# Wider, differently paced weight conversions, and an SBUF copy under the second ELU half, in a float32 attention and two-MoE kernel

## The chip, the cores and the metric

The kernel runs on one core of one Trainium2 chip. The metric is the device time of one execution in microseconds (us). Runs of the same kernel are compared by their median.

## The reference, cut to what matters

Three blocks follow each other: a linear attention, an MLP with an ELU, and a mixture of four experts with a ReLU. All are float32; the two ELU weights `w_in` and `w_out` come as 64-bit floats and are converted on the chip.

```python
def phi(x):                                   # 4 batches, 8 heads, 576 rows, 64 -> 128 features
    proj = einsum('bhsd,df->bhsf', x, w_phi)
    proj = proj - max(abs(proj), axis=-1)
    return concatenate([exp(proj), exp(-proj)])
num = phi(q) @ (phi(k)^T v);  den = phi(q) @ sum(phi(k)) + 1e-6
x = num / den                                 # as 2304 rows of 512
h = x @ w_in                                  # 512 -> 2048
x = where(h > 0, h, exp(min(h, 0)) - 1) @ w_out
for e in range(4):                            # w1: 512 -> 1024, w2: 1024 -> 512
    out += p[:, e] * (maximum(x @ w1[e], 0) @ w2[e])
```

## The kernel before, in words

Every float32 product is made of three products of a rounded high part and a low part (`hi*hi`, `hi*lo`, `lo*hi`), which ScalarE (a copy to the type fp32r) and VectorE or GpSimd (a subtraction) split off. Names of engines below: PE is TensorE, DVE is VectorE, ACT is ScalarE, POOL is GpSimd, SP issues the DMAs.

**Stage 1, attention, ELU first half and conversions** (to about 461 us). `attention` (L344) runs 16 pairs of heads as generators (`pair`, L175), several in flight. For each pair DVE makes two projections safe (`guard`, L205: a reduction L208 and a subtraction L209; the results for q are the tiles `qd0` and `qd1`), PE transposes them (L248), ACT takes exponentials, PE forms `kv` and `num`, DVE divides (a reciprocal L329 and products L332). The first half of the 2048 ELU features is done in 9 tiles of 256 rows by 4 units (`Elu`, L491: first product L503 to L505, ELU L511 to L516, second product L532 to L534).

In the same stage `convert64` (L99) turns `w_in` and `w_out` from 64-bit floats into float32, 32 tiles of 128x512: it loads 64-bit words into the tile `w64` (L101), takes absolute values on ACT (L107), clamps, shifts, and rebuilds the high word on DVE (L109 to L111), makes a power of two from it on DVE (L112, tile `pw`), scales the low word on ACT (L113, tile `low`), multiplies and adds on POOL (L115, L117). The 16 tiles of the first half are split into high and low parts (L121, L123); the 16 tiles of the second half are written to DRAM (`wscr`, L119) and read back later. A block is 256 columns (`CVW`), so there are 64 blocks. The pool `cv` has three buffers of each tile (`CVB`), so up to three blocks are in flight; the buffer of `w64` comes free for the next load when L111 and L113 have read it.

**What sets the order.** The generator `weight_stream` (L413) advances the blocks in flight by one step per call. `drive` and `slot` (L736, L751) call it `wrate` times at each of four points of an ELU unit, and the loop at L763 calls it `PRE` times per attention step; `need_w` forces what is due. The resulting program order is a priority: a scheduler of the framework then places the instructions of each engine, taking into account which buffers are free. On the chip each engine runs its own queue strictly in that order.

**Stage 2, ELU second half** (about 461 to 676 us). The second half of the features is done with a seven-product (Winograd) form of 2x2 blocks on groups of 768 rows (`Up`, L614). Each `UpElu` (L667) forms sums of PSUM banks and kept copies: `middle` and `end` write the sum of a kept copy and a bank back into the bank (L647, L664), or into the SBUF tile `c22` (L656), or use the bank as it is (L662); `half` (L668) then reads this sum twice: ACT makes `relu(-c)` and `exp` in the tile `te` (L671, L672), DVE makes `max(te - 1, c)` (L673), ACT and DVE split it into `h` (L674, L675). The bank is in use until L673 has read it. PSUM has eight banks; four to eight of them hold the sums of `Out` (L678, L696 to L698).

**Stage 3, experts** (676 us to the end). The same `Up` with a ReLU (`half`, L632), and `Down` (L704) for the second product.

Of the kernel before, what the change touches and what calls it, by code (L numbers as in the profile page):

```python
# [19 lines left out]
P = 128  # L20
# [13 lines left out]
TC = 384  # L34
# [8 lines left out]
ATT_LAG = 5  # L43
PRE = 2
RATE = 1.4
# [3 lines left out]
ATE = 6  # L49
WFAST = 4  # L50
TEB = 2
PB = 4
EL = 'V'
NF32 = 7
LDB = 1
CVP = 16
CVW = 256
CVOFF = 0
# [5 lines left out]
def attn_elu_moe_kernel(ctx: ExitStack, tc: tile.TileContext, kq_in, vv, w_phi, w_in, w_out, probs, w1, w2, out):  # L64
# [34 lines left out]
    def convert64(dst, src, adder):  # L99
# [4 lines left out]
        top = cv.tile([P, CVW], U32, tag="top", name="top")  # L104
        pw = cv.tile([P, CVW], U32, tag="pw", name="pw")
        low = cv.tile([P, CVW], F32, tag="low", name="low")
        A.activation(f32(top), f32(hi), ACTF.Abs)  # L107
# [3 lines left out]
        V.scalar_tensor_tensor(out=top, in0=hi, scalar=0xC0000000, in1=top, op0=ALU.bitwise_and, op1=ALU.bitwise_or)  # L111
        V.tensor_scalar(out=pw, in0=top, scalar1=0xFF800000, scalar2=None, op0=ALU.bitwise_and)  # L112
        A.activation(low, lo, ACTF.Copy, scale=2.0 ** -52)  # L113
        yield
        G.tensor_tensor(out=low, in0=low, in1=f32(pw), op=ALU.mult)  # L115
        yield
        adder.tensor_tensor(out=f32(top), in0=f32(top), in1=low, op=ALU.add)  # L117
        if dst.dtype == F32:
# [495 lines left out]
    class Up:  # L614
# [16 lines left out]

        def half(self, c, s, f):  # L632
            h = hp.tile([P, 2, TC], F32R, tag="h", name="h", bufs=HB)
            A.activation(h[:, 0], c, ACTF.Relu)  # L634
            V.scalar_tensor_tensor(out=h[:, 1], in0=c, scalar=0.0, in1=f32(h[:, 0]), op0=ALU.max, op1=ALU.subtract)  # L635
            hs[s, f] = h
# [6 lines left out]
        def middle(self):  # L643
            q = self.q
            b2 = bank()[:, :TC]
            self.product(b2, 2, 2)
            V.tensor_tensor(out=b2, in0=self.m, in1=b2, op=ALU.add)  # L647
            self.half(b2, 0, q)
            self.product(self.b1, 3, 4, True)
            self.ma = self.keep(self.b1, "cma")  # L650
            self.b3 = bank()[:, :TC]
            self.product(self.b3, 4, 3)
            self.product(self.b1, 1, 1, True)
            mab = self.keep(self.b1, "cmab")
            c22 = hp.tile([P, TC], F32, tag="c22", name="c22", bufs=1)
            V.tensor_tensor(out=c22, in0=mab, in1=self.b3, op=ALU.add)  # L656
            self.half(c22, 1, q + NQ)

        def end(self):
            q = self.q  # L660
            self.product(self.b1, 5, 5, True)
            self.half(self.b1, 0, q + NQ)  # L662
            self.product(self.b3, 6, 6, True)
            V.tensor_tensor(out=self.b3, in0=self.ma, in1=self.b3, op=ALU.add)  # L664
            self.half(self.b3, 1, q)

    class UpElu(Up):  # L667
        def half(self, c, s, f):  # L668
            h = hp.tile([P, 2, TC], F32R, tag="h", name="h", bufs=HB)
            t = bp.tile([P, TC], F32, tag="te", name="te", bufs=TEB)  # L670
            A.activation(t, c, ACTF.Relu, scale=-1.0)  # L671
            A.activation(t, t, ACTF.Exp, scale=-1.0)  # L672
            V.scalar_tensor_tensor(out=t, in0=t, scalar=1.0, in1=c, op0=ALU.subtract, op1=ALU.max)  # L673
            A.activation(h[:, 0], t, ACTF.Copy)  # L674
            on[EL].tensor_tensor(out=h[:, 1], in0=t, in1=f32(h[:, 0]), op=ALU.subtract)  # L675
            hs[s, f] = h
# [59 lines left out]
    def slot():  # L736
        quota[0] += rate[0]
        while quota[0] >= 1:
            quota[0] -= 1
            if done[0] < limit[0]:  # L740
                next(stream, None)
        for _ in range(wrate[0]):
            next(weights, None)

    wrate = [WRATE]
    quota = [0.0]
# [21 lines left out]
    for t, u in order(TAIL):  # L768
        if u == 0:
# [3 lines left out]
            limit[0] = NP * (t // 2 + 2)  # L773
            rate[0] = RATE if t < ATE else 0.0
            if t == ATE:
                att.close()
# [164 lines left out]
```

## Time and profile before

| | us |
|---|---|
| median of 3 runs (lowest, highest) | 1435.88 (1433.95, 1436.28) |
| the profiled execution's own time | 1437.87 |
| span of the profiled execution | 1436.1 |
| PE busy | 1376.5 |
| DVE busy | 751.3 |
| ACT busy | 644.1 |
| POOL busy | 448.9 |

The span runs from the first to the last instruction. A wait is listed as who waited, on which line, for whom; the share of busy time of an engine is given for stretches of the span. PE's rows are its matmuls, PEld's are the weight loads, which overlap them.

### The profile page before, as it was taken

The page shows a single profiled execution, that of the slowest core. Times are in us where ns is not written, and L with a number is a line of the kernel's source. Part 1 is how long each engine was busy: PE and PEld are TensorE (multiplying, and loading weights), DVE is VectorE, ACT ScalarE, POOL GpSimd, SP SyncE. Part 2 cuts the span into 40 slices and gives each one's busy share as a digit, 9 for nine tenths or more (in the row PEclk, how much of TensorE's full clock was granted, in tenths as well). Part 3 has the DMA queues.
Part 4 walks back from the last instruction along what each step waited for, and adds up shares of the span by engine and source line. Part 5 has one row for each costly group of instructions (what it writes and reads, how often), then busy time and mean ns, then how long its engine had stood idle before and what let it go on. Part 6 is the DMA issues. An engine that isn't in the chain of part 4 may idle for free.

```text
span 1436.1 us, 21373 instructions
## 1 busy us (share of the span) xinstructions
PE 1376.5 (96%) x8040; PEld 1271.6 (89%) x8040; DVE 751.3 (52%) x1253; ACT 644.1 (45%) x1436; POOL 448.9 (31%) x506
## 2 busy tenths in 40 slices
PE   7899889799999999999999999999999999999998
PEld 6789889799999999989888989898988989889897
DVE  7988998776564464575434333233433334323332
ACT  6777767666555645484333443122431214322121
POOL 5567777655325220254111341001330004300000
PEclk9999989999999999999999999999999999999999
DMA  5433443421132331337333223534154362433421
GB/s 157 130 112 121 138 137 113 132 87 42 48 113 78 92 99 45 117 121 244 126 138 121 104 74 126 192 107 154 44 162 155 102 213 59 140 110 132 157 85 66
DMA packets 98360, 168.55 MB, mean 117 GB/s; under 512 B 28113, under 2 KB 45649, under 8 KB 98257
## 3 DMA queue, kind: packets, MB, share of 16 engines
q1 hardware_dynamic: 98256, 167.19, 35.3%
q8 instruction: 63, 1.03, 0.3%
q14 instruction: 41, 0.33, 0.1%
HBM read 113.41 MB, written 53.74 MB: 116 GB/s over the span
## 4 chain that ended last, share of the span: by engine, by line
PE 64%; DMA 3%; DVE 3%; ACT 1%; issue 1%; POOL 1%; SPq 0%; DVEq 0%; POOLq 0%; ACTq 0%
PE bank L623 9%; PE bank L624 9%; PE bank L625 9%; PE bank L719 9%; PE bank L721 9%; PE bank L720 9%; PE bank L696 2%; PE bank L697 2%; PE bank L698 2%; DMA wst<-in_w 1%; PE bank L533 1%; PE bank L534 1%; PE bank L532 1%; DMA y<-yscr 1%; PE bank L504 1%
## 5 line engine op out<-in xcount | busy, mean ns | idle before, releaser
L623 PE MATMUL bank<-xv,w 128*128 128x384 f32 x840 | 279.3, 337 | 6.0 <-DVE c L656 2.8
L624 PE MATMUL bank<-xv,w 128*128 128x384 f32 x840 | 281.6, 335 | 0.0
L625 PE MATMUL bank<-xv,w 128*128 128x384 f32 x840 | 277.3, 335 | 0.0
L719 PE MATMUL bank<-w,h 128*128 128x512 f32 x576 | 226.3, 396 | 1.8 <-ACT h L634 1.8
L720 PE MATMUL bank<-w,h 128*128 128x512 f32 x576 | 226.7, 394 | 0.0
L721 PE MATMUL bank<-w,h 128*128 128x512 f32 x576 | 201.5, 395 | 0.0
L465 POOL TENSOR_TENSOR w<-wst,w 128x256 fp32r<-128x256 f32 x100 | 76.7, 787 | 383.9 <-ACT w L464 368.9
L623 PEld LDWEIGHTS bank<-xv,w 128*128 128x128 f32 x840 | 157.7, 188 | 17.5 <-DVE c L656 3.1
L624 PEld LDWEIGHTS bank<-xv,w 128*128 128x128 f32 x840 | 157.8, 188 | 4.8
L625 PEld LDWEIGHTS bank<-xv,w 128*128 128x128 f32 x840 | 157.4, 188 | 0.0
L635 DVE SCALAR_TENSOR_TENSOR h<-bank,h 128x384 fp32r<-128x384 f32 x144 | 77.0, 554 | 122.8 <-ACT h L634 122.7
L634 ACT ACTIVATE h<-bank 128x384 fp32r<-128x384 f32 x144 | 66.7, 489 | 156.8 <-PE bank L625 94.0
L719 PEld LDWEIGHTS bank<-w,h 128*128 128x128 f32 x576 | 108.1, 188 | 25.5 <-ACT h L634 3.1
L720 PEld LDWEIGHTS bank<-w,h 128*128 128x128 f32 x576 | 108.1, 188 | 22.3
L721 PEld LDWEIGHTS bank<-w,h 128*128 128x128 f32 x576 | 107.0, 188 | 21.9 <-DVE h L635 1.4
L629 ACT ACTIVATE cmab<-bank 128x384 f32<-128x384 f32 x60 | 29.4, 491 | 187.8 <-PE bank L625 187.8
L574 POOL TENSOR_TENSOR xv<-xs,xv 128x768 fp32r<-128x768 f32 x24 | 46.1, 1925 | 192.1 <-ACT xv L573 184.2
L647 DVE TENSOR_TENSOR bank<-cm,bank 128x384 f32<-128x384 f32 x60 | 33.6, 560 | 131.6 <-PE bank L625 117.8
L656 DVE TENSOR_TENSOR c<-cmab,bank 128x384 f32<-128x384 f32 x60 | 33.2, 553 | 126.1 <-ACT cmab L629 126.0
L629 ACT ACTIVATE cm<-bank 128x384 f32<-128x384 f32 x60 | 29.4, 490 | 136.4 <-PE bank L625 136.4
L533 PE MATMUL bank<-gl,w 128*128 128x256 f32 x288 | 81.9, 288 | 4.0 <-POOL gl L516 2.6
L503 PE MATMUL bank<-xh,w 128*128 128x256 f32 x288 | 83.2, 290 | 0.4 <-DVE qd L209 0.4
(124 smaller groups left out, 3072.4 us busy)
## 6 DMA issues: line engine op xcount, KB each, us to landing
xv<-xvd SPq DMA_DIRECT2D x42, 768.0 KB, 4.4
wst<-in_w SPq DMA_DIRECT2D x64, 256.0 KB, 2.9
xvd<-xv SPq DMA_DIRECT2D x21, 768.0 KB, 4.3
yscr<-y SPq DMA_DIRECT2D x54, 256.0 KB, 2.6
y<-yscr SPq DMA_DIRECT2D x54, 256.0 KB, 3.0
w<-in_w_in SPq DMA_DIRECT2D x32, 256.0 KB, 3.1
w<-in_w_out SPq DMA_DIRECT2D x32, 256.0 KB, 3.0
kq<-in_kq SPq DMA_DIRECT2D x16, 320.0 KB, 3.6
```

Source lines behind the costliest of these rows:

```text
L465: on[WL[v % len(WL)]].tensor_tensor(out=lo, in0=x, in1=f32(hi), op=ALU.subtract)
L503: PE.matmul(ph[:, j], w[:, 0, c], xh[:, kc], start=(kc == 0), stop=False)
L533: PE.matmul(o, w[:, 0, c], self.gl[:, j], start=False, stop=False)
L623: PE.matmul(o, hi[:, c], x[:, 0, kc], start=not more and kc == 0, stop=False, skip_group_check=more)
L624: PE.matmul(o, hi[:, c], x[:, 1, kc], start=False, stop=False, skip_group_check=more)
L625: PE.matmul(o, lo[:, c], x[:, 0, kc], start=False, stop=kc == 1, skip_group_check=more)
L629: A.activation(c, ps, ACTF.Copy)
L634: A.activation(h[:, 0], c, ACTF.Relu)
L635: V.scalar_tensor_tensor(out=h[:, 1], in0=c, scalar=0.0, in1=f32(h[:, 0]), op0=ALU.max, op1=ALU.subtract)
L719: PE.matmul(self.acc, h[:, 0, c], w[:, 0], start=f == 0, stop=False)
L720: PE.matmul(self.acc, h[:, 0, c], w[:, 1], start=False, stop=False)
L721: PE.matmul(self.acc, h[:, 1, c], w[:, 0], start=False, stop=f == 2 * NQ - 1)
```

## The change

Two edits are made together. In the conversion, a block is 512 columns, so there are 32; the two extra tiles are gone, since the power of two is written over the high words of `w64` and the scaled low word over its low words (every second element), and the product is made there too; so `w64` is in use until POOL's addition, now the last to read it. Its pacing is one call where it was two, then 0.8 from tile 1 on, and 2.5 from tile 6 on (before: 4). In the ELU second half, every sum, and the bank used as it was, goes first to one of two SBUF buffers `c22` (an addition that now writes SBUF, or a copy on DVE), and all later steps work there.

```diff
-PRE = 2
+PRE = 1
-WFAST = 4
+WEARLY = 1.0
+WSLOW = 0.8
+WFAST = 2.5
+CB = 2
-CVW = 256
+CVW = 512
@@ convert64
-        pw = cv.tile([P, CVW], U32, tag="pw", name="pw")
-        low = cv.tile([P, CVW], F32, tag="low", name="low")
...
-        V.tensor_scalar(out=pw, in0=top, scalar1=0xFF800000, scalar2=None, op0=ALU.bitwise_and)
-        A.activation(low, lo, ACTF.Copy, scale=2.0 ** -52)
-        yield
-        G.tensor_tensor(out=low, in0=low, in1=f32(pw), op=ALU.mult)
-        yield
-        adder.tensor_tensor(out=f32(top), in0=f32(top), in1=low, op=ALU.add)
+        V.tensor_scalar(out=hi, in0=top, scalar1=0xFF800000, scalar2=None, op0=ALU.bitwise_and)
+        A.activation(f32(lo), lo, ACTF.Copy, scale=2.0 ** -52)
+        yield
+        G.tensor_tensor(out=f32(lo), in0=f32(lo), in1=f32(hi), op=ALU.mult)
+        yield
+        adder.tensor_tensor(out=f32(top), in0=f32(top), in1=f32(lo), op=ALU.add)
@@ class Up: half becomes out, which makes the sum itself
+        def out(self, x, ps, s, f):
+            c = ps
+            if s and f >= NQ:
+                c = hp.tile([P, TC], F32, tag="c22", name="c22", bufs=CB)
+            if x is not None:
+                V.tensor_tensor(out=c, in0=x, in1=ps, op=ALU.add)
...
@@ class UpElu(Up)
-        def half(self, c, s, f):
+        def out(self, x, ps, s, f):
+            c = hp.tile([P, TC], F32, tag="c22", name="c22", bufs=CB)
+            if x is None:
+                V.tensor_copy(c, ps)
+            else:
+                V.tensor_tensor(out=c, in0=x, in1=ps, op=ALU.add)
...
-            V.scalar_tensor_tensor(out=t, in0=t, scalar=1.0, in1=c, op0=ALU.subtract, op1=ALU.max)
-            A.activation(h[:, 0], t, ACTF.Copy)
-            on[EL].tensor_tensor(out=h[:, 1], in0=t, in1=f32(h[:, 0]), op=ALU.subtract)
+            V.scalar_tensor_tensor(out=c, in0=t, scalar=1.0, in1=c, op0=ALU.subtract, op1=ALU.max)
+            A.activation(h[:, 0], c, ACTF.Copy)
+            V.tensor_tensor(out=h[:, 1], in0=c, in1=f32(h[:, 0]), op=ALU.subtract)
@@ slot
-        for _ in range(wrate[0]):
+        wquota[0] += wrate[0]
+        while wquota[0] >= 1:
+            wquota[0] -= 1
             next(weights, None)
...
+            if t == 1:
+                wrate[0] = WSLOW
```

The program order that results is shown at two places, on DVE. The first is the twelfth of the sixteen attention pairs, where DVE makes `qd0` and `qd1`, which PE's transposes read. Before:

```order
L514 SCALAR_TENSOR_TENSOR g_3418<-g_3418,bank_3341 128x512
L332 TENSOR_TENSOR xf_3229<-bank_3318,rc_3230 64x288
L332 TENSOR_TENSOR xf_3229<-bank_3319,rc_3230 64x288
L109 TENSOR_SCALAR top_3799<-top_3799 128x256
L110 TENSOR_SCALAR top_3753<-top_3753 128x256
L111 SCALAR_TENSOR_TENSOR top_3669<-w64_3667,top_3669 128x256
L209 TENSOR_TENSOR qd0_3093<-bank_3273,mx_3280 128x512
L209 TENSOR_TENSOR qd1_3094<-bank_3354,mx_3361 128x512
```

and now:

```order
L329 RECIPROCAL rc_2786<-rc_2786 128x288
L208 TENSOR_REDUCE mx_2831<-bank_2824 128x4
L332 TENSOR_TENSOR xf_2785<-bank_2787,rc_2786 64x288
L332 TENSOR_TENSOR xf_2785<-bank_2788,rc_2786 64x288
L209 TENSOR_TENSOR qd0_2665<-bank_2824,mx_2831 128x512
L329 RECIPROCAL rc_2786<-rc_2786 128x288
L208 TENSOR_REDUCE mx_2903<-bank_2896 128x4
L332 TENSOR_TENSOR xf_2785<-bank_2867,rc_2786 64x288
L332 TENSOR_TENSOR xf_2785<-bank_2868,rc_2786 64x288
L209 TENSOR_TENSOR qd1_2666<-bank_2896,mx_2903 128x512
```

The conversions (`top`, L109 to L112) that stood between the attention's instructions are gone from this place. Counted over DVE's whole queue, the conversion blocks that are complete ahead of the 5th, 7th, 10th, 12th and 13th `qd1` were 16, 29, 47, 56 and 63 of 64; now they are 13, 21, 32, 32 and 32 of 32.

The second place is the start of the ELU second half on DVE; L674, L672, L679 and L681 are now the sum, the copy, the maximum and the low part of `h` (before L647, L656 and L664; none; L673; L675). Before:

```order
L647 TENSOR_TENSOR bank_5919<-cm_5852,bank_5919 128x384
L673 SCALAR_TENSOR_TENSOR te_5928<-te_5928,bank_5919 128x384
L647 TENSOR_TENSOR bank_6012<-cm_5978,bank_6012 128x384
L675 TENSOR_TENSOR h_5927<-te_5928,h_5927 128x384
L656 TENSOR_TENSOR c22_5957<-cmab_5955,bank_5942 128x384
L673 SCALAR_TENSOR_TENSOR te_5960<-te_5960,c22_5957 128x384
L664 TENSOR_TENSOR bank_5942<-cma_5940,bank_5942 128x384
L673 SCALAR_TENSOR_TENSOR te_5987<-te_5987,bank_5845 128x384
L675 TENSOR_TENSOR h_5959<-te_5960,h_5959 128x384
```

and now:

```order
L674 TENSOR_TENSOR c22_5398<-cm_5324,bank_5391 128x384
L679 SCALAR_TENSOR_TENSOR c22_5398<-te_5401,c22_5398 128x384
L674 TENSOR_TENSOR c22_5430<-cmab_5428,bank_5415 128x384
L681 TENSOR_TENSOR h_5400<-c22_5398,h_5400 128x384
L672 COPY c22_5459<-bank_5317 128x384
L679 SCALAR_TENSOR_TENSOR c22_5430<-te_5433,c22_5430 128x384
L681 TENSOR_TENSOR h_5432<-c22_5430,h_5432 128x384
L679 SCALAR_TENSOR_TENSOR c22_5459<-te_5462,c22_5459 128x384
L674 TENSOR_TENSOR c22_5474<-cma_5413,bank_5415 128x384
```

Each bank is now read once, by a sum or a copy that writes `c22`; before, L673 was the last to read it, after two instructions of ACT. The number of instructions on DVE rises by the copies, 12 in all.

## Rows read from the trace of the kernel before

**Rows 1.** The page: busy time of the engines.

```profile
PE 1376.5 (96%) x8040; PEld 1271.6 (89%) x8040; DVE 751.3 (52%) x1253; ACT 644.1 (45%) x1436; POOL 448.9 (31%) x506
```

**Rows 2.** Busy time by stretch, (x) instructions; then granted clock, DMA share, GB/s.

```profile
0.00:36.00 36.00, 27.73 (x148) 23.86 (x148) 27.97 (x60) 22.55 (x53) 18.62 (x30) 0.95 0.54 157
36.00:81.00 45.00, 39.40 (x229) 34.52 (x230) 44.48 (x83) 34.43 (x89) 26.83 (x39) 0.97 0.43 128
81.00:217.00 136.00, 123.23 (x907) 117.17 (x907) 122.40 (x221) 94.04 (x229) 100.62 (x124) 0.96 0.41 126
217.00:302.00 85.00, 73.31 (x576) 70.96 (x576) 71.72 (x125) 56.72 (x134) 58.02 (x67) 0.95 0.39 119
302.00:372.00 70.00, 70.00 (x587) 69.71 (x586) 45.71 (x65) 47.00 (x106) 30.98 (x34) 1.00 0.17 55
...
461.00:676.00 215.00, 205.37 (x1160) 200.22 (x1158) 124.88 (x197) 119.19 (x253) 67.02 (x59) 0.99 0.37 121
676.00:1436.00 760.00, 750.32 (x3716) 668.56 (x3714) 266.36 (x450) 222.01 (x478) 111.80 (x119) 1.00 0.36 123
```

**Rows 3.** PE's waits, 217 to 302 us: total, times, longest.

```profile
PE bank L248 <- DVE qd L209: 10.5, 4, 8.3
```

**Rows 4.** DVE's conversion groups, 217 to 302 us: busy, mean ns, idle before.

```profile
L109 DVE TENSOR_SCALAR top<-top 128x256 f32<-128x256 f32 x15 | 9.3, 618 | 4.9 <-ACT top L107 4.3 <-POOL el L271 0.5
L111 DVE SCALAR_TENSOR_TENSOR top<-w,top 128x256 uint32<-128x256 uint32 x17 | 9.1, 549 | 0.1
L110 DVE TENSOR_SCALAR top<-top 128x256 uint32<-128x256 uint32 x17 | 8.9, 532 | 0.1
L112 DVE TENSOR_SCALAR pw<-top 128x256 uint32<-128x256 uint32 x16 | 6.8, 439 | 0.0
```

**Rows 5.** Single lines, whole span: ns min/median/max, first and last start.

```profile
L109 DVE TENSOR_SCALAR top<-top x64: 223/294/1469, 8.8 to 296.3; 128x256 f32<-128x256 f32 x64
L111 DVE SCALAR_TENSOR_TENSOR top<-w,top x64: 360/425/1515, 10.6 to 301.0; 128x256 uint32<-128x256 uint32 x64
L112 DVE TENSOR_SCALAR pw<-top x64: 276/283/1355, 12.3 to 302.1; 128x256 uint32<-128x256 uint32 x64
L516 DVE TENSOR_TENSOR gl<-g,gh x24: 678/693/1735, 260.4 to 464.2; 128x512 fp32r<-128x512 f32 x24
L516 POOL TENSOR_TENSOR gl<-g,gh x12: 1268/1318/1467, 93.3 to 247.6; 128x512 fp32r<-128x512 f32 x12
L117 POOL TENSOR_TENSOR top<-top,low x64: 721/735/1070, 13.6 to 306.3; 128x256 f32<-128x256 f32 x64
```

**Rows 6.** PE's and PEld's waits, 461 to 676 us.

```profile
PE bank L696 <- DVE te L673: 6.4, 5, 1.8
PE bank L623 <- DVE te L673: 1.1, 3, 0.4
PEld bank L696 <- DVE te L673: 8.0, 5, 2.1
PEld bank L623 <- DVE te L673: 2.0, 3, 0.7
```

**Rows 7.** DVE groups, 461 to 676 us.

```profile
L675 DVE TENSOR_TENSOR h<-te,h 128x384 fp32r<-128x384 f32 x48 | 37.0, 772 | 19.9 <-ACT h L674 19.1
L673 DVE SCALAR_TENSOR_TENSOR te<-te,bank 128x384 f32<-128x384 f32 x36 | 19.7, 546 | 1.9 <-ACT te L672 1.7
L673 DVE SCALAR_TENSOR_TENSOR te<-te,c 128x384 f32<-128x384 f32 x12 | 7.1, 595 | 5.8 <-ACT te L672 5.8
L664 DVE TENSOR_TENSOR bank<-cma,bank 128x384 f32<-128x384 f32 x12 | 6.7, 555 | 0.8 <-PE bank L625 0.5
```

**Rows 8.** SP's queue waits, 0 to 302 us.

```profile
SPq L101 <- DVE top L111: 101.5, 50, 8.0
```

**Rows 9.** The page's DMA issues: KB each, median us from issue to landing.

```profile
w<-in_w_in SPq DMA_DIRECT2D x32, 256.0 KB, 3.1
xv<-xvd SPq DMA_DIRECT2D x42, 768.0 KB, 4.4
```

More of the change, by code (lines that the diff above doesn't have):

```diff
@@ L49 @@
 ATE = 6
-WFAST = 4
+WEARLY = 1.0
+WSLOW = 0.8
+WFAST = 2.5
+CB = 2
 TEB = 2
 PB = 4
-EL = 'V'
 NF32 = 7
@@ L646, in middle @@
             self.product(b2, 2, 2)
-            V.tensor_tensor(out=b2, in0=self.m, in1=b2, op=ALU.add)
-            self.half(b2, 0, q)
+            self.out(self.m, b2, 0, q)
             self.product(self.b1, 3, 4, True)
@@ L654, in middle @@
             mab = self.keep(self.b1, "cmab")
-            c22 = hp.tile([P, TC], F32, tag="c22", name="c22", bufs=1)
-            V.tensor_tensor(out=c22, in0=mab, in1=self.b3, op=ALU.add)
-            self.half(c22, 1, q + NQ)
+            self.out(mab, self.b3, 1, q + NQ)
         def end(self):
@@ L661, in end @@
             self.product(self.b1, 5, 5, True)
-            self.half(self.b1, 0, q + NQ)
+            self.out(None, self.b1, 0, q + NQ)
             self.product(self.b3, 6, 6, True)
-            V.tensor_tensor(out=self.b3, in0=self.ma, in1=self.b3, op=ALU.add)
-            self.half(self.b3, 1, q)
+            self.out(self.ma, self.b3, 1, q)
     class UpElu(Up):
-        def half(self, c, s, f):
+        def out(self, x, ps, s, f):
[4 more added lines that the diff above has]
+                V.tensor_tensor(out=c, in0=x, in1=ps, op=ALU.add)
             h = hp.tile([P, 2, TC], F32R, tag="h", name="h", bufs=HB)
@@ L741, in slot @@
                 next(stream, None)
-        for _ in range(wrate[0]):
+        wquota[0] += wrate[0]
+        while wquota[0] >= 1:
+            wquota[0] -= 1
             next(weights, None)
-    wrate = [WRATE]
+    wrate = [WEARLY]
+    wquota = [0.0]
     quota = [0.0]
```

## The prediction

> **What bounds the kernel now.** I read the page's busy times first: PE is busy for 1376.5 us of the 1436.1 us span, DVE for 751.3 [rows 1]. No edit here changes the number of PE's matmuls, so the change can only win back time in which PE starves. Busy time by stretch says where that is [rows 2]. From 676 us on PE is busy 750.3 of 760 us; what idles there is the start and the tail, and the change hardly touches it. From 302 to 372 us, with attention and ELU units still running but no conversions left, PE is busy 70.0 of 70. In the 85 us before that, 217 to 302, it idles 11.7 us, and its weight loads, which run back to back when PE is fed, idle 14.0. DVE is busy 71.7 us of those 85, against 45.7 of 70 in the stretch after. From 36 to 81 us DVE is busy 44.5 of 45 us. So DVE holds the first 302 us.
>
> The waits name the place: from 217 to 302 us PE's transposes wait 10.5 us for DVE's `qd`, 8.3 of it in one wait [rows 3]. They wait because DVE's queue is in order and conversions stand ahead of `qd` in it: in this stretch the four conversion instructions take 9.3 + 9.1 + 8.9 + 6.8 = 34.1 us of DVE [rows 4]. Many of them take far longer than they need: L109 has a median of 294 ns and a mean of 618 here, at most 1469 in the span [rows 4, 5].
>
> In the ELU second half (461 to 676 us) PE idles 9.6 us and the weight loads 14.8 [rows 2]. There PE waits 6.4 + 1.1 us for L673, and the weight loads 8.0 + 2.0 [rows 6]. L673 does not make `h`; it is the last reader of the PSUM bank, so these are waits for a free bank.
>
> **The change part by part.** *(a) The late conversions go.* By the order of DVE's queue, 17 of the 64 blocks were still to come behind the tenth `qd1`, which in the trace ends at about 217 us; now none is. DVE loses its 34.1 us of conversions in 217 to 302 us, and keeps 71.7 - 34.1 = 37.6 us of work in 85 us, a lower share than in 302 to 372 us, where PE does not idle. So the stretch should look like the next one: it gives back the 14.0 us that the weight loads idle. The granted clock adds a little: 0.95 over 85 us is 8.5 us at the lower of its two levels, 1.2 GHz, after stalls, and work there takes twice as long; with half of that time filled, 4 us. I take 15. Bounds: 8, if only the 8.3 us wait goes, and 18.
>
> *(b) The same conversions come earlier and cost less each.* A block of 256 columns takes DVE, at the medians, 0.294 + 0.294 + 0.425 + 0.283 = 1.30 us (L110 taken as L109) [rows 5]. At 512 columns, a two-input instruction takes 0.693 (L516) against 0.425 at 256, so 256 columns more cost it 0.27 us. The one-input ones start 0.13 us below it at 256 columns, half of 0.27, so I take half the slope: 0.294 + 0.13 = 0.42. A block of 512 is then 3 x 0.42 + 0.69 = 1.95 us. Ahead of the tenth `qd1` that makes 32 x 1.95 = 62.4 us against 47 x 1.30 = 61.1: nothing gained, nothing lost. But ahead of the fifth, which ends at about 81 us, it is 13 x 1.95 = 25.4 against 16 x 1.30 = 20.8, and in 36 to 81 us DVE has 0.5 us free [rows 2]. So PE falls behind by some 4.6 us early, and can make up a part where DVE is less full (122.4 of 136 us in 81 to 217). I take 3 us lost. The bounds come from the 512-column cost, which no row shows with a result written to every second element: if it is twice the 256-column one, 32 x 2.60 = 83.2, 22 us more; below, see the next paragraph.
>
> Beside these medians stands waiting: per block the means exceed the medians, in 217 to 302 us by 0.32, 0.24, 0.12 and 0.16 us for the four [rows 4, 5], and the worst, 1.469 us, is a free instruction plus most of one GpSimd subtraction of 1.318. A GpSimd instruction of a conversion grows from 0.735 to about 1.32 us (L516 on POOL) [rows 5], while the conversion instructions on DVE ahead of the tenth `qd1` fall from 47 x 4 = 188 to 32 x 4 = 128. Each waits up to 1.8 times as long, a third fewer wait: I count no change. If each waited as long as now, a third of it would go: at their mean of 0.21 us, 60 x 0.21 = 12 us less, the lower bound. The Trainium skill, page SBUF — State Buffer, section Who interferes with whom, speaks against the wider block: a VectorE instruction with two SBUF inputs or in its two-port mode shares a port with GpSimd, and the one that issues second is held for the whole of the other instruction. The trace agrees, with L109's 294 and 1469 ns; by that rule the 12 us are not to be had.
>
> *(c) The ELU second half.* The bank is now free after one sum or copy of DVE, instead of after the sum, two instructions of ACT and L673. The waits for L673 go: 7.5 us by PE, 10.0 by the weight loads. I take 8; bounds 0 (below) and 14.8, all the idle time of the loads. Added are 12 copies; a sum of a bank takes 0.555 us [rows 7], so 12 x 0.555 = 6.7 us of DVE, beside 215 - 124.9 = 90 us in which it idles [rows 2]; without that cover it would cost those 6.7. ACT reads SBUF instead of PSUM, beside 96 us of idle time. What is late next is `h` itself, behind the maximum, ACT's copy and the subtraction.
>
> *(d) At no cost:* a second `c22` in the experts, and the pace of 2.5, since need and room in the ring of weights set that stage's order: the weight splits stand at the same places among ACT's ELU instructions as before.
>
> Sum: -15 + 3 - 8 = -20 us. The sum is made against the profiled execution, 1437.87 us (span 1436.1 and 1.8 around it), which gives 1417.9; it lies 2.0 above the median of 1435.88. As a median: **1416 us**.
>
> **The rivals.** *A. The bank comes free, but the wait moves to `h`.* In the ELU half L679 and L681 both read two SBUF tiles. L673 took 546 ns on average with a bank as an input and 595 with `c22`, L675, always on SBUF, 772 [rows 7]; POOL is busy 67 of the 215 us. If the 36 that now read `c22` went to 772, that is 36 x 0.226 = 8.1 us more on the chain that makes `h`, as much as (c) gains. Then only (a) and (b) are left: 1435.9 - 12 = 1424. The rule of the Trainium skill named above (page SBUF — State Buffer, Who interferes with whom) is this rival's: L673 with a bank has one SBUF input, L679 has two. Against it: DVE idles 90 us there, and the order puts more first products between. Chance 0.20.
>
> *B. Width saves nothing.* If 512 columns cost twice 256 columns, the early part loses the bound of (b), 22 us, and -15 + 22 - 8 = -1: 1435. For it speaks that L112, the scaling and the product now work on every second element; against it, L111 reads every second element already, at 425 ns, and L516 shows the fixed part. Chance 0.12.
>
> *C. Slower: the load buffer's round.* SP waits 101.5 us, 50 times for 64 loads, for L111 to free a `w64` [rows 8]; so three buffers pace the loads. Now POOL's addition frees it. From 9 to 217 us, 47 blocks in 3 buffers are 15.7 rounds of 13.3 us; 32 blocks are 10.7 rounds, with 19.5 us for each. A round grows by the load (3.1 us for 256 KB, 4.4 for 768 KB [rows 9], so by up to 1.3), by 0.65 on DVE, by two GpSimd instructions of 1.32 and by some 0.6 of ACT: 18.5 us, only 1.0 below. Beyond 19.5 every microsecond makes L109 late 10.7 times, and `qd` stands behind L109. From a round of 21.4 us on the whole gain is eaten; at 23 us (both GpSimd instructions 2.2 us longer, for their strided data or behind others, POOL being busy 100.6 of 136 us) it costs 3.5 x 10.7 = 37 us: 1436 - 20 + 37 = 1453. Against it: the round now contains waiting in DVE's queue, which need not grow. Chance 0.11.
>
> **How the numbers follow.** Chances: forecast 0.57 (its own range 1406 to 1425), A 0.20, B 0.12, C 0.11. A measurement of this kernel can tell some 0.2%, 3 us. Forecast and A are faster; of B, around 1435, 0.03 is faster, 0.06 the same and 0.03 slower; C is slower: faster 0.80, same 0.06, slower 0.14. The range takes in forecast, A and the lower half of B, and on the other side the bounds of (a) and (c) together with a part of the 12 us: 1404 to 1434. Left out are C, half of B and the far ends.
>
> **What would show it.** Right: from the tenth `qd1` on no conversion on DVE, and no wait of PE's transposes for `qd` of over 1 us up to 372 us; conversion instructions of 512 columns with medians of about 0.42 and 0.69 us; in the ELU half no wait of PE for the maximum (L679) as a bank's last reader, and under 3 us idle. Wrong: PE idle before 217 us up by 10 us or more, medians of 0.59 and 0.85 (B), SP's waits for L117 and DVE's for L107 of over 20 us (C), or waits of the second product (now L702) for the low part of `h`, L681 (A).

## The result: 0.5% slower, and the profile after

The changed kernel takes 1442.62 us (median of 4 runs, 1440.81 to 1444.55), the one before 1435.38 (1433.95 to 1436.28): a ratio of 1.0052, 95% interval 1.0034 to 1.0069. The forecast was 1416, the range ended at 1434. The profiled execution has a span of 1439.0 us and a time of 1440.81, the fastest of the four, so it shows 2.9 of the 7.2 us by which the medians differ; the rest must be read from the experiments.

Busy time by stretch of the changed kernel (PE, PEld, DVE, ACT, POOL with the count of instructions; granted clock, DMA share, GB/s), to be laid beside [rows 2]:

```profile
0.00:36.00 36.00, 21.46 (x107) 17.97 (x108) 27.72 (x47) 21.82 (x42) 19.16 (x23) 0.96 0.58 168
36.00:81.00 45.00, 36.91 (x220) 33.09 (x220) 41.81 (x63) 30.65 (x67) 29.56 (x27) 0.92 0.46 144
81.00:217.00 136.00, 120.23 (x858) 112.76 (x857) 122.44 (x174) 91.86 (x196) 98.97 (x85) 0.96 0.47 147
217.00:302.00 85.00, 84.01 (x700) 83.23 (x699) 54.55 (x76) 56.74 (x125) 46.07 (x48) 1.00 0.24 78
302.00:372.00 70.00, 70.00 (x588) 69.71 (x587) 46.25 (x64) 48.69 (x108) 29.00 (x33) 1.00 0.16 52
461.00:676.00 215.00, 203.74 (x1137) 198.86 (x1137) 132.03 (x203) 119.05 (x249) 67.14 (x56) 0.98 0.36 114
676.00:1436.00 760.00, 750.92 (x3721) 669.35 (x3719) 268.56 (x454) 221.78 (x478) 111.74 (x119) 1.00 0.36 124
```

Two things stand in it. From 217 to 302 us PE gains 84.01 - 73.31 = 10.7 us, but before 217 it loses 190.36 - 178.60 = 11.8 (sums of the first three lines), more than the 10 us that the prediction named as a sign of being wrong. And from 461 to 676 us, where 8 us were to be won, PE is busy 1.6 us less than before and idles 11.3 us, where under 3 were to show the forecast right.

DVE tells the same story from its side. From 0 to 217 us it is busy 191.97 us, against 194.85 before; from 217 to 302 it is 54.55 against 71.72. So of the 20 us of DVE's time that the wider conversions save in 302 us, 17 come up as idle time in the late stretch, where DVE no longer holds anything. In the first 217 us it is nearly as full as it was, and with fewer of the attention's instructions done.

PE's waits of 0 to 81 us (total, times, longest), first before, then with the change:

```profile
PE bank L248 <- DVE qd L209: 8.8, 5, 2.8
PE bank L220 <- DMA wbd<-in_w_phi: 4.0, 1, 4.0
PE bank L241 <- ACT kp L213: 0.8, 1, 0.8
```

```profile
PE bank L248 <- DVE qd L209: 15.6, 4, 5.7
PE bank L220 <- DMA wbd<-in_w_phi: 4.0, 1, 4.0
PE bank L320 <- ACT kvw L290: 3.0, 2, 1.8
```

The wait for `qd` nearly doubles early. From 217 to 302 us it is down from the 10.5 us of [rows 3] to

```profile
PE bank L248 <- DVE qd L209: 1.0, 2, 0.5
```

In the ELU second half (461 to 676 us) the waits of [rows 6] for L673 are gone, as forecast, and others stand in their place, here of PE and then of its weight loads:

```profile
PE bank L623 <- DVE c L674: 4.7, 2, 3.0
PE bank L623 <- ACT cmab L629: 3.2, 3, 2.0
PE bank L702 <- ACT h L680: 2.1, 2, 1.4
PE bank L623 <- ACT cma L629: 0.6, 1, 0.6
PE bank L623 <- DVE c L672: 0.5, 1, 0.5
...
PEld bank L623 <- DVE c L674: 5.9, 4, 3.4
```

L623 opens a bank for the next first product; the last reader of that bank is now the sum L674 itself, and PE waits for it up to 3.0 us. DVE's timeline around the longest of these waits (start, duration, instruction, idle time before it and what ended it) shows why the sum is late:

```profile
610.12 0.56 DVE L674 TENSOR_TENSOR c<-cmab,bank 128x384 f32<-128x384 f32 x1 [0.73 <-ACT cmab L629]
611.49 0.56 DVE L672 COPY c<-bank 128x384 f32<-128x384 f32 x1 [0.81 <-PE bank L625]
611.96 0.55 DVE L679 SCALAR_TENSOR_TENSOR c<-te,c 128x384 f32<-128x384 f32 x1
613.58 0.63 DVE L681 TENSOR_TENSOR h<-c,h 128x384 fp32r<-128x384 f32 x1 [1.06 <-ACT h L680]
614.56 0.51 DVE L452 TENSOR_TENSOR wtmp<-wst 128x256 f32<-128x256 f32 x1 [0.36 <-DMA wst<-in_w]
614.99 0.55 DVE L679 SCALAR_TENSOR_TENSOR c<-te,c 128x384 f32<-128x384 f32 x1
615.46 0.54 DVE L674 TENSOR_TENSOR c<-cma,bank 128x384 f32<-128x384 f32 x1
```

At 610.12 and 611.49 a sum and a copy fill the two `c22`. The third, `cma` plus its bank, has no `c22` until L681, the last reader of the first one, has run; L681 waits 1.06 us for ACT's L680, and a difference of weight blocks (L452) that waits for its DMA stands between as well. The sum starts at 615.46 and PE goes on at 616.06. The bank is free sooner after its sum, but the sum itself comes later.

### The profile page after: what moved, and what is told of

Its sections match the earlier page's. It is cut to its first block, busy times and chain, and to the rows that moved or that the text cites. A ratio compares the mean times of both kernels' runs of the same rounds, so it can differ in the third digit from the quotient of the medians.

```text
span 1439.0 us, 20985 instructions
## 1 busy us (share of the span) xinstructions
PE 1374.3 (96%) x8040; PEld 1271.3 (88%) x8040; DVE 741.4 (52%) x1137; ACT 638.0 (44%) x1356; POOL 437.2 (30%) x426
## 4 chain that ended last, share of the span: by engine, by line
PE 60%; DMA 4%; issue 3%; DVE 2%; POOL 2%; ACT 1%; SPq 0%; DVEq 0%; POOLq 0%; ACTq 0%
PE bank L623 9%; PE bank L624 9%; PE bank L625 9%; PE bank L725 9%; PE bank L727 8%; PE bank L726 8%; PE bank L702 2%; PE bank L703 2%; PE bank L704 2%; DMA wst<-in_w 1%; POOL w L465 1%; DMA y<-yscr 1%; DMA yscr<-y 1%; POOL w L477 1%; PE bank L533 0%
## 5 line engine op out<-in xcount | busy, mean ns | idle before, releaser
L623 PE MATMUL bank<-xv,w 128*128 128x384 f32 x840 | 279.6, 337 | 11.1 <-DVE c L674 4.7
L623 PEld LDWEIGHTS bank<-xv,w 128*128 128x128 f32 x840 | 157.9, 188 | 22.3 <-DVE c L674 5.9
L639 ACT ACTIVATE h<-bank 128x384 fp32r<-128x384 f32 x144 | 66.7, 489 | 159.6 <-PE bank L625 94.2
L629 ACT ACTIVATE cmab<-bank 128x384 f32<-128x384 f32 x60 | 29.4, 491 | 184.5 <-PE bank L625 184.5
L637 DVE TENSOR_TENSOR bank<-cm,bank 128x384 f32<-128x384 f32 x48 | 26.9, 560 | 120.8 <-PE bank L625 104.7
L629 ACT ACTIVATE cm<-bank 128x384 f32<-128x384 f32 x60 | 29.4, 489 | 133.2 <-PE bank L625 133.1
L637 DVE TENSOR_TENSOR c<-cmab,bank 128x384 f32<-128x384 f32 x48 | 26.6, 554 | 113.8 <-ACT cmab L629 113.8
L532 PE MATMUL bank<-gh,w 128*128 128x256 f32 x288 | 79.6, 288 | 5.1 <-ACT gh L515 5.1
```

The costliest lines, as they stand in the source:

```text
L532: PE.matmul(o, w[:, 0, c], self.gh[:, j], start=start, stop=False)
L623: PE.matmul(o, hi[:, c], x[:, 0, kc], start=not more and kc == 0, stop=False, skip_group_check=more)
L629: A.activation(c, ps, ACTF.Copy)
```

## The experiments

The profiled executions, by times read from their traces (us from the start of the span; the half with its transition is the sixth line less the fourth):

| | before | change | e1 ELU alone | e2 conv. alone | e9 | e5 |
|---|---|---|---|---|---|---|
| 5th `qd1` ends | 81.1 | 95.5 | 81.2 | 97.4 | 97.7 | 97.2 |
| 10th `qd1` ends | 217.0 | 232.0 | 216.8 | 235.2 | 235.8 | 235.6 |
| 13th `qd1` ends | 302.2 | 298.7 | 302.6 | 301.9 | 302.5 | 302.3 |
| ELU first half ends on PE | 471.0 | 468.8 | 471.8 | 471.9 | 472.6 | 471.8 |
| last output product of the ELU half | 671.0 | 671.8 | 674.9 | 670.0 | 667.9 | 667.2 |
| first down product of the experts | 676.5 | 680.1 | 683.3 | 675.4 | 676.4 | 673.6 |
| half with transition | 205.5 | 211.3 | 211.5 | 203.5 | 203.8 | 201.8 |

Each kernel was timed in 5 rounds against the kernel before, whose median over these batches was 1437.3 to 1437.9 us. The change has two independent parts, so each was run alone first.

**e1: the ELU half alone**, with the conversions and their pace of before.

```diff
 CVW = 256   CVB = 3   (own scratch tiles pw, low; pace of before)
+class Up, class UpElu: as in the change, CB = 2
```

> The kernel before with the ELU half's edit alone (sums and the copy go to two SBUF buffers); every engine's order up to the ELU half is as before. Theory 1 (the bank comes free earlier but the sum now waits for a c22 buffer, which is free only after the low part of h): 2 to 6 us slower than before, 1437 to 1441. Theory 2 (the forecast's: waits for a bank go, nothing replaces them): 1427 to 1430.

Measured: 1443.83 us, ratio 1.0039 (1.0026 to 1.0052). The ELU half alone makes the kernel slower by about as much as the whole change does. The first theory has the direction, and its range ends 2.8 us too low; PE's waits from 461 to 676 us repeat those above line for line (L674 4.7 us in two, L629 for `cmab` 3.3, L680 2.1).

**e2: the conversions alone**, in place, 512 columns, with the new pace; the ELU half of before.

```diff
-CVW = 256   -own scratch tiles pw, low
+CVW = 512   +in place in w64, WEARLY 1.0, WSLOW 0.8, WFAST 2.5
 class Up, class UpElu: as before
```

> The changed kernel with the ELU half of before, so the conversion's edit alone. Theory 1 (what conversions lose ahead of the tenth qd1, 15 us, is given back by their absence behind it, 18 us): 1432 to 1436. Rival (the conversions are the whole slowdown): 1440 to 1444.

Measured: 1437.45 us, ratio 1.0000 (0.9990 to 1.0009), between the two ranges and 1.5 us above the first. 18 us are lost at the tenth `qd1`, and they are all back at the thirteenth: the table's early loss and late gain are the same size. So the conversions change nothing in all that could be measured, and the 2.2 us by which the change's profiled execution leads at the end of the first half are not theirs: e2, e5 and e9, with the same conversions, end it at 471.8 to 472.6.

**e8: in place, but 256 columns**; **e7: 512 columns with two load buffers**; **e14: 256 columns with six**; **e16: 512 columns with one.** All with the ELU half of before. They separate a block's width from the number of blocks that the order can put ahead of the attention's work. The pace of e8 and e14 is that of e2, doubled for blocks half as wide.

```diff
 (e2 with)
+CVW = 256   CVB = 3   PRE = 2, WEARLY = 2.0, WSLOW = 1.6     # e8
+CVW = 512   CVB = 2                                 # e7
+CVW = 256   CVB = 6   PRE = 2, WEARLY = 2.0, WSLOW = 1.6     # e14
+CVW = 512   CVB = 1                                 # e16
```

> The conversion of the change with its in-place tiles and pace, but with blocks of 256 columns, ELU half of before. Theory 1 (the width decides): as before, 1433 to 1438, and the fifth qd1 ends at 81 us, as before. Rival (the in-place form decides, since the load buffer is held until GpSimd's addition): the fifth qd1 ends at 90 us or later, 1440 or more.

> The conversion's edit alone with two blocks in flight instead of three, ELU half of before: 10 instead of 13 blocks stand ahead of the fifth qd1, 25 instead of 32 ahead of the tenth. Theory 1 (too many conversions too early on DVE): the fifth qd1 ends at 86 to 90 us instead of 95, total 1426 to 1432. Rival (each wide GpSimd instruction holds DVE for longer, wherever it stands): within 2 us of the run with three in flight.

> The conversions in place in blocks of 256 columns with six load buffers, the ELU half as before; the order then puts 28 blocks of 256 ahead of the fifth qd1 (14 of 512 in width, the change has 13) and all 64 ahead of the ninth. Theory 1: the number of columns that the buffers let the order put ahead of the first pairs makes the early loss, whatever the width of a block; then the fifth qd1 ends at 95 to 101 us, and PE's wait for qd from 217 to 302 us is under 2 us, as in the change. Theory 2: it is the width, with one long block and long GpSimd instructions before each qd; then the fifth qd1 ends at 84 to 91 us. In all 1437 to 1444, since narrow blocks cost DVE 25 us more than wide ones.

> The conversions of the change with one load buffer, the ELU half of before; the order then puts 5 blocks of 512 ahead of the fifth qd1 (10 with two buffers, 13 with three) and 20 ahead of the tenth (25, 32). Theory 1: the number of columns ahead sets the early loss; then the fifth qd1 ends at 80 to 85 us, the tenth at 212 to 219, and the late conversions cost what they save: 1433 to 1438. Theory 2: with one buffer each load's round stands in DVE's queue before L109; then DVE waits over 20 us for ACT's L107 up to 302 us and the time is 1440 or more.

| | blocks ahead of the 5th / 10th `qd1`, in 512 columns | 5th `qd1` | 10th | 13th | time, ratio (interval) |
|---|---|---|---|---|---|
| before, 256 x 3 | 8 / 23.5 | 81.1 | 217.0 | 302.2 | |
| e16, 512 x 1 | 5 / 20 | 81.4 | 247.1 | 317.6 | 1462.17, 1.0179 (1.0164 to 1.0195) |
| e8, 256 x 3 | 8 / 23 | 83.2 | 220.6 | 306.7 | 1442.82, 1.0028 (1.0015 to 1.0040) |
| e7, 512 x 2 | 10 / 25 | 91.0 | 221.1 | 300.1 | 1435.18, 0.9982 (0.9971 to 0.9992) |
| e2, 512 x 3 | 13 / 32 | 97.4 | 235.2 | 301.9 | 1437.45, 1.0000 (0.9990 to 1.0009) |
| e14, 256 x 6 | 14 / 32 | 103.2 | 249.8 | 318.4 | 1454.19, 1.0114 (1.0095 to 1.0132) |

Blocks ahead are counted in the order of DVE's queue. From 8 blocks ahead of the fifth `qd1` on, the early loss follows the number of columns that stand ahead, at either width: narrow blocks that stand as far ahead lose more (103.2), not less. With 5 ahead nothing more is won (81.4). Width itself is a gain: at nearly the same place in the order, e14 and e2 differ by 16.7 us. And putting the blocks further ahead is a loss: e14 is 11.4 us above e8; e2 is 2.3 above e7, where the two intervals just overlap. Windows of e14, against those of the change above:

```profile
0.00:36.00 36.00, 23.18 (x114) 20.41 (x115) 28.48 (x62) 24.33 (x60) 22.30 (x34) 0.88 0.58 181
36.00:81.00 45.00, 32.55 (x175) 29.30 (x174) 44.45 (x91) 31.35 (x83) 30.88 (x44) 0.80 0.41 129
81.00:217.00 136.00, 116.08 (x773) 107.33 (x772) 128.26 (x245) 87.39 (x218) 96.88 (x127) 0.92 0.49 148
217.00:302.00 85.00, 81.09 (x657) 80.49 (x656) 50.79 (x74) 54.65 (x125) 46.39 (x49) 0.96 0.22 66
```

DVE is busy 201 of the first 217 us and then has 34 of 85 us free. PE idles 12.5 us of 36 to 81 us and meets a granted clock of 0.80 there, between its two levels, 1.2 and 2.4 GHz: part of the stretch, after stalls, ran at the lower one. PE's wait for `qd` from 217 to 302 us is 1.2 us, as the first theory said. The fifth `qd1` is 2.2 us and the total 10 us above its ranges: its direction held, its price was too low.

e7 gains, but less than was expected: its fifth `qd1` ends at 91.0 us and not by 90, 7 of its 32 blocks stand behind the tenth, and it lies 2.3 us from e2, where the rival allowed 2. e16 met the first theory at the fifth `qd1` (81.4) and the second from then on: up to 302 us DVE waits 36.6 us for ACT's L107, which follows the load, so with one buffer each load's round stands in DVE's queue. What neither theory named is who pays: the weights of the first ELU units come too late. From 81 to 217 us DVE's longest wait, PE's, and the stretch itself:

```profile
DVE top L109 <- ACT top L107: 27.9, 9, 6.6
```

```profile
PE bank L532 <- ACT w L121: 20.9, 4, 5.7
PE bank L503 <- ACT w L121: 10.9, 2, 5.6
```

```profile
81.00:217.00 136.00, 102.88 (x677) 94.51 (x676) 74.39 (x121) 72.62 (x149) 71.05 (x66) 0.81 0.27 86
```

So the blocks have a due time on one side (the ELU's weights, and a load's round that DVE must not stand behind) and cost PE on the other (DVE's queue); two buffers lie between. e8 is a miss: in place at 256 columns it should have been as fast as before. It is 4 us slower (0.28%), in the rival's range, with its blocks at nearly the same places in the order (8 and 23 ahead, before 8 and 23.5); but its fifth `qd1` ends at 83.2 us and not at the rival's 90. In it SP waits 27 times, 35.8 us in all up to 302 us, for POOL's L117 to free a `w64`, while L111 freed it before [rows 8], and 55.9 us, before 22.5, to send off what L117 made (L119). That these waits are the cause was not tried.

**e6: e2 with each GpSimd instruction cut into two of 256 columns.**

```diff
-        G.tensor_tensor(out=f32(lo), in0=f32(lo), in1=f32(hi), op=ALU.mult)
+        for c in (slice(0, CVW // 2), slice(CVW // 2, CVW)):
+            G.tensor_tensor(out=f32(lo)[:, c], in0=f32(lo)[:, c], in1=f32(hi)[:, c], op=ALU.mult)
 (the addition and the subtraction in the same way)
```

> The conversions of the change with the ELU half of before; each GpSimd instruction of a conversion is cut into two of 256 columns, DVE's and ACT's stay at 512. Theory 1: wide GpSimd instructions hold DVE's conversion instructions longer, 12.1 us of holding up to the fifth qd1 in the change against 6.8 before; then the holding falls to 7 to 9 us and the fifth qd1 ends at 91 to 94 us instead of 97. Theory 2: the loss up to there is the number of blocks that the order puts ahead of it (13 against 8), and holding is a side effect; then the fifth qd1 ends at 96 us or later, since GpSimd now does more instructions. Either way the loss is given back later: 1435 to 1439 in all.

Measured: 1441.83 us, ratio 1.0028 (1.0015 to 1.0042); the fifth `qd1` ends at 100.6. The holding of DVE's conversion instructions falls a little (11.2 us over 58 instructions, 0.19 each, against 13.1 over 53, 0.25 each, in e2), the fifth `qd1` gets no earlier (14 blocks stand ahead of it), and POOL is busy 15 us longer up to 390 us (244.5 against 229.4). The time of the fifth `qd1` is the second theory's. The holding up to there fell too little to test the first one. Over the whole kernel it did fall: the rows of the four lines L109 to L112 add up to 90.5 us, against 100.2 in e2, and yet the kernel is 4 us slower. So less holding alone, bought with more work on POOL, gains nothing. The loss is not all given back, against what was expected of both.

**e9: the change with the maximum written to `te`**, so that a `c22` is free as soon as L679 has read it; **e5: the change with three `c22`** and three `part` buffers instead of four.

```diff
-            V.scalar_tensor_tensor(out=c, in0=t, scalar=1.0, in1=c, op0=ALU.subtract, op1=ALU.max)
+            V.scalar_tensor_tensor(out=t, in0=t, scalar=1.0, in1=c, op0=ALU.subtract, op1=ALU.max)
 (L680 and L681 read t)                                                   # e9
-CB = 2   PB = 4
+CB = 3   PB = 3                                                          # e5
```

> The change whole, but the maximum's result goes to te instead of back into c22, so that a c22 is free once the maximum has read it, and not only after ACT's copy and the subtraction. Theory 1: the ELU half lost because two c22 buffers, each held until the low part of h is made, make the next sum or copy wait behind that chain in DVE's queue, and with it PE; then PE's waits for c (L674, L672) of up to 3.2 us in 461 to 680 us fall to under 1 us, the half takes 198 to 200 us instead of 203, and the time is 1436 to 1440. Theory 2: the loss is the added DVE work (copies, two SBUF inputs) and the later start of the experts, whatever the buffers; then the half stays at 203 and the time at 1441 to 1445.

> The change whole with three c22 buffers instead of two, for which one of the four part buffers is given up. Theory 1 (two c22 buffers, held through the whole ELU chain, stop the sums): PE's waits for c fall as in the run beside it, the half takes 198 to 200 us, and the time is 1436 to 1440, unless the missing part buffer makes the sums of the outputs late (waits of L725 or of the last L707 over 3 us). Theory 2 (added DVE work): as the change, 1441 to 1445.

Measured: e9 1435.97 us, ratio 0.9988 (0.9977 to 0.9998); e5 1434.26, 0.9978 (0.9966 to 0.9990). Both do every copy and every sum of the change, and the slowdown is gone: the half with its transition takes 203.8 and 201.8 us instead of 211.3. The half ends on PE 195.3 us (e9) and 195.4 (e5) after the first half, in the change 203.0 and in e1 203.1. Before it is 200.0, but the seven traces with the ELU half of before (this one, e2, e6, e7, e8, e14, e16) spread from 198.1 to 200.4, and with the transition from 203.5 to 206.0. Both times are at or below the lower edge of the first theory's. PE's waits from 461 to 676 us, first in e9, then in e5:

```profile
PE bank L623 <- ACT cmab L629: 3.3, 3, 2.2
PE bank L623 <- DVE c L672: 1.5, 1, 1.5
PE bank L702 <- DVE c L672: 0.9, 1, 0.9
...
PE bank L623 <- DVE c L674: 0.4, 2, 0.2
```

```profile
PE bank L623 <- ACT cmab L629: 3.3, 3, 2.2
PE bank L623 <- DVE c L672: 3.0, 3, 2.6
```

The 4.7 us for L674 are down to 0.4 and to nothing worth a line; the 2.1 us for L680 are gone. The waits for the copy (L672) have grown from 0.5 us to 2.4 and 3.0, though the first theory had all waits for `c` fall under 1 us. From the end of the first half to the end of the second PE idles 6.8 us in e9 (195.3 less 188.5 busy), in the change 11.3 (203.0 less 191.7), at a granted clock of 0.99 and 0.98. DVE's timeline of e9 at the same step of the program:

```profile
613.09 0.56 DVE L672 COPY c<-bank 128x384 f32<-128x384 f32 x1 [0.81 <-PE bank L625]
613.57 0.55 DVE L679 SCALAR_TENSOR_TENSOR te<-te,c 128x384 f32<-128x384 f32 x1
614.22 0.56 DVE L674 TENSOR_TENSOR c<-cma,bank 128x384 f32<-128x384 f32 x1
615.18 0.65 DVE L681 TENSOR_TENSOR h<-te,h 128x384 fp32r<-128x384 f32 x1 [0.41 <-ACT h L680]
```

The sum of `cma` follows L679 at once and stands ahead of L681: 1.1 us after the copy instead of 4.0.

**e11, e13, e15: the findings put together**, each on the change: e11 with two load buffers and e9's edit, e13 with two load buffers and e5's, e15 with all three.

```diff
-CVB = 3                       +CVB = 2                                   # e11, e13, e15
+maximum written to te                                                    # e11, e15
+CB = 3   PB = 3                                                          # e13, e15
```

> The change with two load buffers for the conversions instead of three (so that the order puts fewer blocks ahead of the first pairs) and with the maximum's result in te. Theory 1: the two-buffer conversions keep their 2 us of gain, and the ELU half its wait-free order: 1431 to 1436. Theory 2 (added DVE work in the ELU half costs its 6 to 7 us, whatever the buffers): 1439 to 1443.

> The change with two load buffers for the conversions, three c22 and three part buffers. Theory 1: the two gains are independent, 2.3 us from the load buffers and 3.2 from the ELU half with three c22: some 5.5 us below the kernel before, 1430 to 1433. Theory 2 (they share a loss, or stage 1's gain is given back before the ELU half ends): 1433 to 1436.

> As the run with two load buffers, three c22 and three part buffers, and the maximum's result in te, so that c22 is free after the maximum. Theory 1 (what stops PE in the ELU half is the time that the sums wait for a c22): the waits for c of 2.7 us that three buffers leave fall to under 1.5 us, 1428 to 1432. Theory 2: what is left are other chains (cmab, the outputs' sums), and it is as the run beside it, within 1 us.

Measured: e11 1432.51 us, ratio 0.9968 (0.9956 to 0.9980); e13 1434.29, 0.9974 (0.9963 to 0.9985); e15 1432.38, 0.9961 (0.9949 to 0.9973). All three beat both kernels. e11 met its first theory. e13 did not add up: it met its second theory and is no better than e5 alone. e15 lies in neither range, 0.4 us above the first theory's and 1.9 below e13, where the second allowed 1. Its waits for `c` (L674, L672), which were to fall, add up to 3.2 us, in e13 to 2.9. So why it is ahead of e13 is open. The intervals of the three overlap, so which of them is best stays open too.

## Why the prediction was wrong, step by step

**(a) The late conversions go: right, a little too small.** 15 us, at most 18, were forecast (the 18 has a slip: 8.5 us at half the clock, half of them filled, give back 2 us, not 4); the stretch from the end of the tenth `qd1` to the end of the thirteenth shrinks from 85.2 to 66.7 us, by 18.5. PE idles 1.0 us of 217 to 302 and the weight loads 1.8, nearly as in the stretch after.

**(b) Earlier and cheaper: the first of the two steps that failed, by 12 us.** It took 3 us lost early, from 4.6 more on DVE ahead of the fifth `qd1`; that `qd1` ends 14.4 us later, the tenth 15.0, so nothing is made up in between. The price of a block, as a sum of free rows, was right. The conversions' lines over the whole span of the change (minimum/median/maximum ns), to be laid beside [rows 5]:

```profile
L109 DVE TENSOR_SCALAR top<-top x32: 358/428/1556, 10.4 to 220.1; 128x512 f32<-128x512 f32 x32
...
L110 DVE TENSOR_SCALAR top<-top x32: 364/590/1561, 11.3 to 220.9; 128x512 uint32<-128x512 uint32 x32
...
L111 DVE SCALAR_TENSOR_TENSOR top<-w,top x32: 622/692/1799, 12.9 to 222.3; 128x512 uint32<-128x512 uint32 x32
...
L112 DVE TENSOR_SCALAR w<-top x32: 360/423/1490, 15.0 to 224.8; 128x512 uint32<-128x512 uint32 x32
```

0.42 and 0.69 us were forecast. L110's median of 0.59 contains waiting: in e16, where little is held, it is 0.43, so L110 is counted here as L109. What failed is what stands beside the medians. Of the 14.4 us at the fifth `qd1`, free durations make 4.8 (20.8 to 25.6 us); the holding, of which the prediction says "I count no change", 5.3 (6.8 us in 66 instructions, now 12.1 in 53: 0.10 to 0.23 each, 2.2 times, not the 1.8 at most that was granted); DVE's idle time 3.2 (8.5 to 11.7, which was put at nothing); and 1.1 the rest.

At the tenth `qd1`, for which that sentence was written, the account is another. The conversions' rows, free durations and holding together, grow only by 4.4 us (93.4 to 97.8; the holding by 2 to 3 of them). DVE's idle time adds 5.5 (22.1 to 27.6). The last 5.1 come from the overlap of rows: rows of DVE begin a little before the row ahead of them ends, so that the 361 rows up to there take 21.5 us less than their sum, and the 298 of the change only 16.4 less. So the sum of row durations, 62.4 against 61.1 us, is no measure of DVE's time where the number of rows falls. The lower bound of 12 us less did not come ahead of the tenth `qd1`, and the upper one of 22 more was the nearer end.

The step's second error is in the frame: it treated (a) as a gain and (b) as its small price. With DVE busy 192 of the first 217 us (before 195), work that is moved ahead of the tenth `qd1` takes the same starvation with it. Up to 302 us PE is busy 263.7 us before and 262.6 in the change, so its idle time is the same in all and only stands elsewhere. e2's 18 us lost and won can be read as one quantity, seen twice.

**The holding.** In e16, with a single block in flight, DVE's conversion instructions run at their free durations up to the sixth pair (0.0 us held); over the whole kernel their 128 rows add up to 72.6 us, against 97.8 in the change. So some 25 us of DVE's conversion time is waiting that goes with the overlap of blocks. In the change each of the 50 conversion rows on DVE that take over 1.3 times their free duration starts while a row of POOL runs, and 20.5 of their 35 us of waiting stand behind POOL's rows of other blocks (L115, L117, L123), the rest behind POOL's work for attention and ELU; before it is 92 of 92 rows, in e16 18 of 18. The Trainium skill, page SBUF — State Buffer, section Who interferes with whom, says that where a VectorE and a GpSimd instruction contend for the shared port pair, the one that issues second is held for the whole of the other; these rows agree with that.

**(c) The ELU half: the second step that failed, by some 14 us; a term was left out.** The waits for L673 as a bank's last reader went, as forecast, and with e9's edit the half shows it: from 472.6 to 667.9 us, 195.3, against 200.0 before, 4.7 us of the 8 forecast (2.8 to 5.1 against the spread above). What was missing, and so put at nothing, is the new buffer's own round. The step asked how long a bank is held and not how long a `c22` is: from its sum through two instructions of ACT, L679 and L680 to L681, with two buffers for the four sums and copies of a unit. That cost 203.0 - 195.3 = 7.7 us in the half. The transition to the experts is 8.3 us in the change against 5.5 before: PE waits 3.1 us for the first `h` of the experts,

```profile
PE bank L725 <- ACT h L639: 3.1, 1, 3.1
```

and the sum behind that `h` (L637) stands in DVE's queue behind outputs' sums (L707) that wait for the DMA of their `part`. In e9 this transition is still 8.5 us, in e5 6.4. DVE's timeline shows why e9's gain does not reach the experts, first before (where L701 and L647 are the outputs' sum and the sum behind `h`), then in e9:

```profile
674.93 0.56 DVE L701 TENSOR_TENSOR part<-bank,part 128x384 f32<-128x384 f32 x1 [0.54 <-DMA part<-x1scr]
675.40 0.55 DVE L647 TENSOR_TENSOR bank<-cm,bank 128x384 f32<-128x384 f32 x1
```

```profile
674.81 0.56 DVE L707 TENSOR_TENSOR part<-bank,part 128x384 f32<-128x384 f32 x1 [0.58 <-DMA part<-x1scr]
675.29 0.55 DVE L637 TENSOR_TENSOR bank<-cm,bank 128x384 f32<-128x384 f32 x1
```

Counted from the end of the first half, the last product of the half ends 4.7 us earlier in e9, but the experts' first sum starts only 1.7 us earlier (675.29 - 472.6 = 202.7, before 675.40 - 471.0 = 204.4), since it stands right behind a sum that waits for its `part`. With the transition e9 takes 203.8 us, within the spread of the ELU half of before, and its time is only 0.12% below before. The best with the transition are e5 and e15, 201.8 and 202.0 us; no run gains the 8 us that were forecast. What would bring `part` sooner was not tried.

The Trainium skill, page VectorE: DVE Perf Modes, section Rules for kernel authors, offers a copy from PSUM to SBUF first where several operations follow. Here a copy or a sum into SBUF costs DVE the 0.55 us that a sum in the bank costs ([rows 7]; L672 and L674 above), so that no time is won on DVE by it, and it pays only as far as the SBUF tile comes free: the half takes 203.1 us in e1, with two tiles held to the end of the chain, and 195.3 in e9, with the same copies.

**(d) The pace and the second `c22` of the experts: nothing, as forecast.** From the first down product to the last the experts take 753.6 us, before 755.1. The pace does little in the first stage either: with 256 columns, three buffers and the pace of e8, the order of PE, DVE, ACT and POOL is as it was, and with 512 columns and three buffers the pace of before or half the new one leaves the same 13, 21, 32, 32 and 32 blocks ahead of the 5th, 7th, 10th, 12th and 13th `qd1` (read from the program order, not from runs). So at these rates the free load buffers, and not the rate at which blocks are offered, decide how many blocks stand ahead: 13 of 32 ahead of the fifth of sixteen pairs.

**The rivals.** A put its 8 us on the read of two SBUF tiles. L679 takes 585 ns and L681 825 on average, against 546 and 772 in [rows 7]: not 226 ns more on each, so its price was wrong. The second product does wait (L702, 2.1 us), but for the high part of `h` (ACT's L680), and the rival named the low one (L681); that wait goes with the `c22` round. B is refuted by the medians of L109, L111 and L112 above; L110's 0.59 is the figure that B named, but its shortest row takes 0.364. C looked at the right ring and at the wrong end of it: SP waits 32.2 us for POOL to free a `w64`, over the 20 that were to show it but far less than the 101.5 of [rows 8], and DVE waits 12.3 us in 7 times for ACT's L107, under the 20 and only 3.6 more than before (8.7):

```profile
SPq L103 <- POOL top L117: 32.2, 14, 5.0
```

```profile
  ACT top L107: 12.3, 7
```

The three buffers do not pace the loads too slowly; at twice the width they let twice as much work into DVE's queue at once. The result lies on C's side of the forecast and comes from no rival: (a) and (b) cancel, and (c) turns from a gain of 8 into a loss of some 6.

## What to carry to other kernels

Where background work shares an in-order engine with the work that feeds PE, ask what decides how much of it may stand ahead: here depth times width of the load ring. Of the conversions tried here, wider blocks with a shorter ring did best, by some 2 us. Look at where the engine that is full gets free time: here the time saved on it came up in a stretch where it no longer held anything, and was worth nothing. When a copy frees one buffer early, write down the round of the buffer that it fills, from its first write to its last reader, with their number, before counting the gain; if the last reader is far away, write the intermediate result somewhere else. And ask what the next stage waits for: here most of what the second half won was lost again behind a transfer.

## What had not been expected of the hardware

A GpSimd product of 512 columns in place on every second element (L115) takes a median of 1044 ns, less than the 1306 of the addition with one dense input and output (L117). Before, with dense tiles of 256 columns, the two took 737 and 735; what makes the difference was not tried.

```profile
L115 POOL TENSOR_TENSOR w<-w x32: 1032/1044/1489, 15.6 to 225.4; 128x512 f32<-128x512 f32 x32
...
L117 POOL TENSOR_TENSOR top<-top,w x32: 1277/1306/1815, 16.7 to 227.7; 128x512 f32<-128x512 f32 x32
```

Rows of DVE overlap: in the timeline above L679 starts at 614.99, 0.08 us before the row of L452 ends (614.56 + 0.51). So merging two instructions into one saves less than the difference of their durations, as in (b): the conversions' rows add up to 128.3 us before and 97.8 now, 30.5 less, but the time that they cover falls from 119.2 to 93.9, by 25.3. The Trainium skill, page Perfetto Trace Analysis, section Optimizing Scalar/DVE Operations, says that the profiled latency of an instruction's fixed overhead is about twice what the engine is busy with it, since the half for the write's acknowledgement overlaps with the next instruction. The overlap of 0.08 us is in keeping with that; how the overhead divides no run here shows.
